# Five stream buffers instead of six, a twelfth kept weight chunk, and eleven zero stores moved from the output phase into the chain

## Chip, cores, metric

One core of one Trainium2 chip. The metric is the device time of one execution in microseconds (us), lower is better. A run more than 1.5% above the fastest of its kernel is called slow, and comparisons use fast runs.

## The reference

Two layers are applied twice, forward and backward, for one token (batch 1, sequence 1): attention over the last 4096 positions of a 32768-long cache (4 groups of 8 heads, head size 128, model width 1024), and an MLP of width 3584 with the mish activation. The kernel returns the output and the gradients of x, both caches and all weights.

```python
x = A_x
x = x + A(layernorm(x), k_cache, v_cache, wq, wo)   # called A1
x = x + B(layernorm(x), w1, b1, w2)                 # B2
x = x + A(layernorm(x), k_cache, v_cache, wq, wo)   # A3
x = x + B(layernorm(x), w1, b1, w2)                 # B4
# out, and the vjp with grad_out: dx, dK, dV, dwq, dwo, dw1, db1, dw2
```

Outside the window, dK and dV are zero: 28672 rows of 4 groups in each, 58.7 MB of zeros that the kernel has to write. It does so in 112 stores of 0.524 MB.

## The kernel before

The vector chain forward and backward (matrix-vector products) needs the weights several times; wq, K and V stay on the chip, 11 of 16 chunks of wo stay (NR), and everything else streams through a ring of six tiles (NB) of 0.524 MB. At the end the weight gradients, all outer products, are made and stored: the output phase. Zero stores are spread over the chain from POOL, each group behind a small copy ("gate") that makes it wait for a chosen value; the rest is stored from SP in the output phase. Cuts are marked.

```python
NB = 6          # ring tiles
NR = 11         # kept chunks of wo
# ...
def st_tile(shape):                  # the next ring tile, in turn
    s = free_order.pop(0)
    free_order.append(s)
    # ...
def bg_zeros(n, after):              # n zero stores from POOL, not before `after` is there
    if n:
        nc.gpsimd.tensor_copy(gate_t[:], after[:, 0:1])
    for _ in range(min(n, len(zero_jobs))):
        nc.gpsimd.dma_start(zero_job(1), zt[:])
# ... mlp_turn: B4 forward and backward over w1, seven blocks of two ring tiles each
for b in range(NBK):
    if b:
        bg_zeros(Z["B4"][b], dh_bf[:, lo0(b):])
    ws[b] = [w1_block(b, hh) for hh in range(2)]      # two loads
    # ... matrix-vector products of block b (PSUM "sm"): first the first half, then the second
    m = mish_exp(hps.cols(0, FB), FB)
    X(b, 0)                          # transposes of the first half, in place
    # ... mish and its derivative
    if b:
        M(b - 1)                     # backward product of block b-1: frees its two tiles
    X(b, 1)
    fill(4, ["wo", "V", "K", "wq"], None, True)       # transposes of kept weights
# ... zero stores of each stage
Z = dict(B2a=1, B2={0: 1, 4: 1, NW2 - 2: 3}, A3=14, B4=[2, 2, 2, 2, 2, 2, 5], A3c=6, A3d=28,
         B4w={1: 1, 4: 1, 7: 1, 10: 1, 12: 2}, W1=0, W1m=(2, 8, 13), A1c=3, A1d=18)
# ... output phase: zeros2(2) at five places, one at the end
```

In attention one ring tile is taken out for scratch, scores and p ("own").

## Time and profile before

| | before |
|---|---|
| time, median of the first 3 runs | 436.23 us (435.78 to 437.06) |
| span of the profiled run (fast) | 437.0 us |
| moved by DMA | 170.13 MB, 389 GB/s on average |
| last evacuation of PSUM ends | 416.1 us |
| from there to the end ("tail") | 20.9 us |

The lines behind these are in the prediction. For comparing kernels I cut the span at marks that every version has, read from the timeline: the start of the layernorms' ln (lnv) and of their backward sums (ab), the start of mish's exponential (u) for w1 blocks 0 and 6, and the end of the last evacuation of an outer product (ops).

### The profile page before, as it was taken

The page shows a single profiled execution, that of the slowest core. Times are in us where ns is not written, and L with a number is a line of the kernel's source. Part 1 is how long each engine was busy: PE and PEld are TensorE (multiplying, and loading weights), DVE is VectorE, ACT ScalarE, POOL GpSimd, SP SyncE. Part 2 cuts the span into 40 slices and gives each one's busy share as a digit, 9 for nine tenths or more (in the row PEclk, how much of TensorE's full clock was granted, in tenths as well). Part 3 has the DMA queues.
Part 4 walks back from the last instruction along what each step waited for, and adds up shares of the span by engine and source line. Part 5 has one row for each costly group of instructions (what it writes and reads, how often), then busy time and mean ns, then how long its engine had stood idle before and what let it go on. Part 6 is the DMA issues. An engine that isn't in the chain of part 4 may idle for free. (4 is left out here: it accounts for less than half of the span.)

```text
span 437.0 us, 11654 instructions
## 1 busy us (share of the span) xinstructions
PE 320.8 (73%) x5010; PEld 218.4 (50%) x5010; DVE 235.8 (54%) x489; ACT 212.5 (49%) x251; POOL 66.2 (15%) x167
## 2 busy tenths in 40 slices
PE   1566746387898998987999478888878797678800
PEld 0343515387474998974797477865431223112100
DVE  3134201086351666782474555556659899899900
ACT  1132100064242686875793242533548787698800
POOL 2000000010530221342242111022501010000000
PEclk9999555575695899997999555999885555555555
DMA  8999999999999799999999999999999999999996
GB/s 316 423 420 415 406 411 383 408 360 372 376 401 353 255 338 363 387 404 407 417 412 377 406 400 386 329 375 414 417 423 392 418 419 412 409 418 418 420 421 290
DMA packets 45057, 170.13 MB, mean 389 GB/s; under 512 B 4529, under 2 KB 11725, under 8 KB 38861
## 3 DMA queue, kind: packets, MB, share of 16 engines
q1 hardware_dynamic: 32752, 125.32, 73.0%
q0 software_dynamic: 12208, 44.06, 25.5%
q8 instruction: 39, 0.64, 0.6%
q14 instruction: 14, 0.11, 0.1%
q10 hardware_dynamic: 44, 0.01, 0.0%
HBM read 70.27 MB, written 99.10 MB: 388 GB/s over the span
## 5 line engine op out<-in xcount | busy, mean ns | idle before, releaser
L282 PEld LDWEIGHTS <-ring 128*128 128x128 bf16 (+2 forms) x1828 | 59.5, 101 | 35.9 <-DMA ring<-in_B_w_dram 11.9
L195 ACT COPY ring<-tps 128x1024 bf16<-128x1024 bf16 (+1 forms) x40 | 37.6, 963 | 27.4 <-PE tps L242 27.3
L185 POOL DMA_DIRECT2D out_dram<-zt x83 | 43.9, 531 | 40.6 <-DMA out_dram<-zt 34.7
L691 ACT COPY ring<-tps 128x1024 bf16<-128x1024 bf16 x28 | 28.3, 1012 | 31.6 <-PE tps L681 24.2
L704 DVE CUSTOM_DVE_ANT_0 ring<-ring,gbc 128x1024 bf16<-128x1024 bf16 x28 | 33.5, 1219 | 16.2 <-PE acc L282 15.1
L242 PE MATMUL tps<-ident_bf,ring 128*128 128x128 bf16 x528 | 38.9, 229 | 4.2 <-DMA ring<-in_B_w_dram 2.9
L282 PE MATMUL ops<-V 2*128 2x512 bf16 (+1 forms) x160 | 31.6, 602 | 7.3 <-DVE K L192 2.1
L195 ACT CAST wq_b<-ops 128x1024 bf16<-128x1024 f32 (+1 forms) x36 | 34.9, 1012 | 3.1 <-PE ops L282 3.0
L242 PEld LDWEIGHTS <-ring 128*128 128x128 bf16 x528 | 32.4, 102 | 6.1 <-DMA ring<-in_B_w_dram 2.5
L282 PEld LDWEIGHTS <-V 128*128 128x128 bf16 (+2 forms) x448 | 16.9, 102 | 33.6 <-issue 31.2
L195 ACT COPY K<-tps 128x1024 bf16<-128x1024 bf16 x17 | 16.8, 1027 | 30.1 <-PE tps L242 30.0
L192 DVE COPY ring<-tps 128x1024 bf16<-128x1024 bf16 (+1 forms) x30 | 19.7, 664 | 21.5 <-PE tps L242 21.5
L192 DVE CAST wq_b<-ops 128x1024 bf16<-128x1024 f32 (+1 forms) x28 | 30.6, 1119 | 0.7 <-PE ops L282 0.7
L282 PE MATMUL ops<-wo_b 2*128 2x512 bf16 x120 | 25.1, 526 | 5.6 <-DVE V L997 1.4
L681 PE MATMUL tps<-ident_bf,ring 128*128 128x128 bf16 x224 | 24.4, 276 | 0.7 <-DMA ring<-in_B_w_dram 0.7
L282 PE MATMUL acc<-a_pair,ring 128*128 128x16 bf16 x448 | 15.9, 172 | 11.5 <-DMA ring<-in_B_w_dram 10.7
L192 DVE COPY K<-tps 128x1024 bf16<-128x1024 bf16 x15 | 10.2, 689 | 24.2 <-PE tps L242 24.1
L192 DVE CAST K<-ops 128x1024 bf16<-128x1024 f32 x16 | 19.5, 1220 | 3.8 <-PE ops L282 3.5
L282 PEld LDWEIGHTS <-wo_b 2*128 2x128 bf16 (+1 forms) x232 | 9.1, 98 | 24.2 <-issue 20.8
L282 PE MATMUL q<-wq_b,nA_pair 128*32 128x512 bf16 x128 | 9.8, 425 | 14.9 <-DMA wq_b<-in_A_wq_dram 14.8
L242 PE MATMUL tps<-ident_bf,K 128*128 128x128 bf16 x256 | 20.2, 240 | 0.5 <-ACT K L195 0.3
L242 PEld LDWEIGHTS <-K 128*128 128x128 bf16 x256 | 17.1, 108 | 6.4 <-issue 5.4
(319 smaller groups left out, 560.7 us busy)
## 6 DMA issues: line engine op xcount, KB each, us to landing
out_dram<-zt POOLq DMA_DIRECT2D x83, 512.0 KB, 9.9
ring<-in_B_w_dram SPq DMA_DIRECT2D x42, 512.0 KB, 8.2
ring<-in_B_w_dram SPq DMA_DIRECT2D x32, 448.0 KB, 6.4
ring<-in_A_wo_dram SPq DMA_DIRECT2D x20, 512.0 KB, 8.0
out_dram<-wo_b SPq DMA_DIRECT2D x10, 1024.0 KB, 11.7
out_dram<-wq_b SPq DMA_DIRECT2D x10, 1024.0 KB, 14.9
out_dram<-zt SPq DMA_DIRECT2D x18, 512.0 KB, 11.0
wq_b<-in_A_wq_dram SPq DMA_DIRECT2D x8, 1024.0 KB, 21.1
```

Of the source, the lines that this page charges most:

```text
L185: nc.gpsimd.dma_start(zero_job(1), zt[:])
L192: nc.vector.tensor_copy(out_ap, in_ap)
L195: nc.scalar.copy(out_ap, in_ap)
L242: nc.tensor.transpose(ps[:, b, :], ap, ident_bf[:])
L282: nc.tensor.matmul(out_ap, lhsT=lhsT, rhs=rhs, start=start, stop=stop, skip_group_check=True, **kw)
L681: nc.tensor.transpose(self.ps[c][:, b, :], w[:, 1, b * P:(b + 1) * P], ident_bf[:])
L691: nc.scalar.copy(self.w[c][:, 1, :], self.ps.pop(c)[:].rearrange("p b c -> p (b c)"))
L704: nc.vector.tensor_tensor_reduce(out=w[:, 0, :], in0=w[:, 0, :], in1=gbc[:], scale=1.0, scalar=0.0, op0=ALU.mult, op1=ALU.add, accum_out=s ...
```

## The change

Intent: a twelfth chunk of wo is kept, so that it isn't streamed again in three of four passes; a ring tile pays for it. And the 11 zero stores of the output phase go into the chain, at places where DMA has holes, so that the output phase has less to store.

```diff
-NB = 6
-NR = 11
+NB = 5
+NR = 12
@@ mlp_fwd
         m = mish_exp(hacc.cols(0, TF), TF)
+        bg_zeros(Z["B2m"], m["y"])
         w2 = W2Pass(a_bf, "wg4")
@@
-    Z = dict(B2a=1, B2={0: 1, 4: 1, NW2 - 2: 3}, A3=14, B4=[2, 2, 2, 2, 2, 2, 5], ..., W1m=(2, 8, 13), A1c=3, A1d=18)
+    Z = dict(B2a=1, B2m=2, B2={4: 1, 10: 1, NW2 - 2: 3}, A3=17, B4=[3, 3, 3, 2, 2, 3, 5], ..., W1m=(2, 5, 8, 11, 13), A1c=3, A1d=19)
@@ output phase
-            16: [lambda: zeros2(2)],
-            22: [finish_rows, lambda: zeros2(2)],
-            26: [finish_rows, lambda: zeros2(2)],
-            32: [lambda: zeros2(2)],
-            40: [lambda: zeros2(2)],
+            22: [finish_rows],
+            26: [finish_rows],
```

(A third line chooses the staging tiles that the ring gives to the output phase; their number stays 14.)

More of the change, by code (lines that the diff above doesn't have):

```diff
@@ L1239, in after_stream @@
     def after_stream():
-        slots.extend(ring_b[:, i * 2048:(i + 2) * 2048] for i in range(0, NB, 2) if own["slot"] not in (i, i + 1))
+        slots.extend(ring_b[:, i * 2048:(i + 2) * 2048] for i in ((0, 2) if own["slot"] == 4 else (0, 3) if own["slot"] == 2 else (1, 3) if own["slot"] == 0 else (3,) if own["slot"] == 1 else (0,)))
     def after_v():
@@ L1251, in put_rows @@
         prep.pop(0)()
-    Z = dict(B2a=1, B2={0: 1, 4: 1, NW2 - 2: 3}, A3=14, B4=[2, 2, 2, 2, 2, 2, 5], A3c=6, A3d=28, B4w={1: 1, 4: 1, 7: 1, 10: 1, 12: 2}, W1=0, W1m=(2, 8, 13), A1c=3, A1d=18)
+    Z = dict(B2a=1, B2m=2, B2={4: 1, 10: 1, NW2 - 2: 3}, A3=17, B4=[3, 3, 3, 2, 2, 3, 5], A3c=6, A3d=28, B4w={1: 1, 4: 1, 7: 1, 10: 1, 12: 2}, W1=0, W1m=(2, 5, 8, 11, 13), A1c=3, A1d=19)
     x1 = None
```

## The prediction

> **What bounds the kernel now.** I read the 40 slices of the page first.
>
> ```profile
> PE   1566746387898998987999478888878797678800
> DVE  3134201086351666782474555556659899899900
> ACT  1132100064242686875793242533548787698800
> DMA  8999999999999799999999999999999999999996
> GB/s 316 423 420 415 406 411 383 408 360 372 376 401 353 255 338 363 387 404 407 417 412 377 406 400 386 329 375 414 417 423 392 418 419 412 409 418 418 420 421 290
> ```
>
> The kernel moves 170.13 MB in 437.0 us, 389 GB/s on average where the best slice reaches 423. The DMA row is 9 nearly everywhere, so DMA looks like the one bound; but GB/s falls to 255-390 in slices 8-16 and 25-26, and in the last ten slices DVE and ACT are as full as DMA. So I cut the span into stages with the table of windows (columns: length, busy time of PE, PEld, DVE, ACT and POOL with counts, clock, DMA share, GB/s).
>
> ```profile
> 60.00:112.00 52.00, 34.31 (x727) 30.07 (x726) 20.70 (x46) 14.88 (x17) 4.17 (x11) 0.57 1.01 381
> 112.00:147.00 35.00, 30.66 (x488) 20.78 (x489) 11.52 (x37) 10.44 (x20) 8.12 (x16) 0.75 1.00 374
> 147.00:150.00 3.00, 3.00 (x76) 3.00 (x74) 2.12 (x7) 1.93 (x3) 1.04 (x3) 1.00 0.13 41
> 150.00:180.00 30.00, 28.30 (x675) 27.60 (x673) 20.91 (x88) 23.85 (x30) 7.28 (x19) 1.00 0.99 356
> 238.00:264.00 26.00, 17.60 (x367) 16.77 (x364) 16.21 (x28) 11.63 (x12) 4.11 (x11) 0.58 1.02 394
> 264.00:292.00 28.00, 23.17 (x460) 22.07 (x461) 13.75 (x27) 10.52 (x13) 2.39 (x7) 0.84 0.99 358
> 338.00:416.00 78.00, 59.89 (x361) 16.61 (x359) 70.69 (x77) 64.51 (x69) 2.83 (x12) 0.50 1.02 416
> 416.00:434.00 18.00, 0.00 (x0) 0.00 (x0) 0.13 (x1) 0.01 (x1) 0.00 (x0) 0.50 0.98 409
> ```
>
> The rows are: first MLP forward (60-112); second attention forward (112-147); the second MLP's w1 blocks, forward and backward (147-180); after the attention backward, the second w2 pass (238-264) and first layer's w1 pass (264-292); the outer products of the output phase (338-416) and its tail, in which all compute is done and DMA drains (416-434). The output phase is full twice: DMA at 416 GB/s, and DVE at 70.69 of 78 us. What it waits for, the waits tell. In that window the lists of waits of DVE and of ACT hold no DMA at all, only each other and PE; so no evacuation is held by a staging buffer. The sync queue's last wait is for the final K stores:
>
> ```profile
> SPq L1425 <- DMA out_dram<-K: 15.0, 1, 15.0
> 416.19 4.39 SPq L1214 DMA_DIRECT2D out_dram<-K  x4
> out_dram<-K SPq DMA_DIRECT2D x4, 1024.0 KB, 14.0
> ```
>
> These K stores, 4 x 1.05 MB, can't be issued before the last evacuation (416), because one staging tile holds all of dK. In the chain I look for PE waiting for loads. Between 147 and 186 that is 0.7 us in two waits; between 238 and 292 it is 10.7 us:
>
> ```profile
> PE acc L282 <- DMA ring<-in_B_w_dram: 7.8, 7, 3.0
> PE tps L242 <- DMA ring<-in_B_w_dram: 2.9, 5, 0.9
> PE sm L282 <- DMA ring<-in_B_w_dram: 0.7, 2, 0.4
> ```
>
> **What the Trainium skill says.** Page "DMA: Bandwidth & Descriptors". Its section "Anatomy of one DMA" gives a fixed cost of about 2.0 us plus bytes at 436 GB/s: 3.2 us for a 524 KB zero store. The trace agrees: the one zero store at 149.1 us, with the queues empty, took 2.9 us. Section "Issuing engines are not separate DMA queues": transfers from SP and from POOL run on the same 16 DMA engines and interleave, so moving zero stores from SP to POOL buys no bandwidth; no slice here exceeds 423 GB/s, whichever queue feeds it. Section "Queues, rings and completion order": each DMA engine alternates between queues by the packet. A w1 block load has rows of 512 elements, 1 KB, a zero store rows of 4 KB, so a load beside zero stores should get far less than half. The trace fits: the same loads took a median of 5.1 us from issue to landing in 135-147, mostly without zeros, and 8.9 us in 146-190, with 19 zero stores.
>
> **The change, part by part.** A chunk or zero store is 0.524 MB, 1.26 us at 416 GB/s.
>
> Kept chunk: wo was loaded 11 + 4 x 5 = 31 times in chunks, now 12 + 4 x 4 = 28: 3 chunks, 1.57 MB, 3.8 us of DMA less, one each in the second forward and the two backward passes. On the engines it is nothing: the instruction order has 16 transposes moved from ring to kept tiles, and 2 of 10 multiply-reduces on DVE gone (1.22 us each, beside other work).
>
> Zero stores: 112 in all. Before, 83 from POOL in the chain, 18 from SP in the last attention backward, 11 from SP in the output phase. After: 94, 18 and 0. The 11 go to the first MLP (+2), second attention forward (+3), the w1 blocks (+4) and the last w1 pass (+2). In the output phase 11 x 1.26 = 13.9 us of DMA vanish. But not 13.9 us of time: compute ends at 416 either way. The wq store issued at 415.06 and the four K stores remain behind it: 5.24 MB, 12.6 us, started about 1.7 us after issue and about 1 us to the last receipt (estimates from the fixed cost above), so landing near 430.4 where now it is 435.6. **Gain at the end: 5.2 us.** The rest of the 13.9 us turns into idle DMA ahead of 416.
>
> Ring of five for six, with one of them scratch during attention: a load is issued when the tile five loads back is free.
> - First MLP: one load less is ahead when the layernorm starts, and one more zero store stands among the loads that count; 2 x 1.26 us against 52 us at 381 for 416 GB/s (4.4 us of slack). I put it at +1.
> - w1 blocks: each needs two tiles and keeps them until the next block is half done. With six tiles both halves of a block come free one block ahead. With five, the second half of block b+1 waits for the first half of block b-1, which M releases some 2.3 us into block b; blocks are 4.4 to 6.5 us long, landings took 8.9 us. DMA share is already 0.99. Added up to the end of the second w2 pass: four zeros, one half not prefetched, one wo chunk less, one prefetch less at the far end: +3 units, **+3.9 us**.
> - Last w1 pass: 2 zeros and a half more, 3.6 us; slack 28 us at 358 for 416, 3.9 us, but PE's 2.9 us of waits there (the transposes, tps, above) show that it is bound by loads already: +1.5.
> - Second attention forward: three zeros less one wo chunk; the 3 us with DMA share 0.13 after it swallow them: 0.
>
> Sum of the shift: +1 + 3.9 + 1.5 = +6.4. That counts nearly no idle DMA as usable. The gates that start each group of zeros (after the mish input, at chunk 4 and 10) are chosen for the holes, so I take about two thirds: **+4**. 436.2 - 5.2 + 4 = **435.0 us**.
>
> **Rivals.** (1) Everything fits in the holes: shift 0, 431.0 us. For it: about 15 us of unused bandwidth in 60-180 (each row's length times what its GB/s lack of 416); against it: the holes lie where the ring is full, and a smaller ring makes them larger. (2) The w1 blocks become bound by load latency: each of five blocks needs about 7 us (2.3 to the release, 4.6-5 to land) for the 5.7 it takes on average now (151.8 to 180.3 in PE's timeline), that is 5 x 1.3 = +6.5, and with contention from three zeros more; with the other terms about 440-442 us. For it: 8.9 us landings. Against: zeros are gated per block, so a late block also delays its competitors. (3) DMA bounds the output phase alone, as its 9s suggest: it would give back the whole 13.9 us and end near 426 with shift 4. Against: DVE and ACT never wait for a DMA there, and the K stores come last.
>
> **Range and chances.** Shift between -1.5 and +10 gives 429.5 to 441, eight in ten. Faster than 427.5 needs a shift below -3.5 or rival 3: 0.05. Slower than 445 needs +14: 0.03. Within 2%: 0.92.
>
> **What would show it.** Right: 168.56 MB moved; last evacuation at 420 +/- 3 instead of 416; last K landing 14-15 us after it instead of 19-20; a DMA hole ahead of it; more PE waits for ring loads at the w1 blocks than 0.7 us. Rival 1: last evacuation near 416. Rival 2: block period near 7 us and some 5 us of ring waits there. Rival 3: evacuations ending before 412. The prediction is wrong outright if evacuations begin to wait for staging tiles, of which the count stays 14, or if the clock granted to TensorE changes a stage.

## The result, and the profile after

| | before | after |
|---|---|---|
| time, median of 4 runs | 436.64 us (435.78 to 440.51) | 454.0 us (449.98 to 459.09) |
| ratio of fast runs | 1 | 1.0349 (95%: 1.0246 to 1.0452) |
| moved | 170.13 MB | 168.56 MB |

Ratios here are the mean time of one kernel's fast runs over that of the other's of the same rounds, so not quite the ratio of the medians. The change is 3.5% slower, outside the predicted range.

The two rows of the changed kernel's page that answer to the slices of before; this profiled run: slow (457.3 us).

```profile
DMA  8999999999999998899999999989998796999978
GB/s 325 420 421 415 408 366 342 375 359 315 376 411 368 366 346 306 315 386 337 412 413 400 381 379 374 316 296 378 415 411 350 298 418 260 392 411 423 378 317 367
```

Less is moved, at a lower rate, 369 GB/s on average; the holes are in the chain (slices 5 to 18 and 25 to 26, counted from 0, as in the prediction) and now in the output phase too. The end of the changed kernel, as a table of windows and the sync queue's timeline and last wait:

```profile
366.00:443.60 77.60, 59.56 (x359) 16.52 (x356) 70.31 (x77) 63.99 (x68) 2.74 (x12) 0.50 0.90 369
443.60:457.00 13.40, 0.00 (x0) 0.00 (x0) 0.00 (x1) 0.00 (x0) 0.00 (x0) 0.50 0.92 382
...
443.66 4.10 SPq L1215 DMA_DIRECT2D out_dram<-K  x4
...
SPq L1423 <- DMA out_dram<-K: 8.2, 4, 2.4
```

The evacuations do the same work in the same time as before (77.6 us here, 78.0 in the matching stretch before); DMA is no longer full beside them (369 for 416 GB/s); the last K stores follow at once, and the tail is 13.7 us instead of 20.9. So the output phase did about what was predicted. All the loss is earlier: the last evacuation ends at 443.6 instead of 416.1.

As that profile is a slow run, I use for the chain the profile of experiment e12, the changed kernel with nothing altered before the dK stores. Stage by stage (us; "A3 fwd" runs to the mish of block 0, "B4 blocks" from block 0 to block 6, "A3 bwd" from there to A3's backward layernorm, "w passes" are the second w2 pass and the last w1 pass, "outputs" runs from A1's backward layernorm to the last evacuation):

| stage | before | after (slow) | e12 (fast) | e12 - before |
|---|---|---|---|---|
| to B2's layernorm | 68.9 | 68.8 | 69.2 | +0.3 |
| B2 | 45.1 | 50.6 | 48.3 | +3.2 |
| A3 fwd | 34.5 | 34.3 | 34.0 | -0.5 |
| B4 blocks | 33.0 | 44.2 | 44.4 | +11.4 |
| A3 bwd | 53.6 | 52.7 | 52.0 | -1.6 |
| w passes | 56.8 | 65.8 | 65.2 | +8.4 |
| A1 bwd | 35.8 | 38.6 | 36.7 | +0.9 |
| outputs | 88.4 | 88.4 | 88.4 | 0 |
| tail | 20.9 | 13.7 | 11.4 (altered) | |
| span | 437.0 | 457.3 | 449.6 | |

Three stages lose 23.0 us, the blocks, the w passes, and B2; the others give 0.9 back, which leaves the 22.1 us by which e12's chain ends later. In all three PE stands still for ring loads. In B2 that was 11.1 us before and 12.8 in e12. These are PE's waits in the changed kernel, at the blocks (147 to 206 us) and in the w passes (250 to 320 us); before it was 0.7 us, and 7.8 + 2.9 us:

```profile
PE sm L282 <- DMA ring<-in_B_w_dram: 10.5, 4, 5.5
...
PE acc L282 <- DMA ring<-in_B_w_dram: 9.6, 7, 3.3
PE tps L242 <- DMA ring<-in_B_w_dram: 8.4, 7, 2.9
```

What one such wait looks like, in e12's timeline of PE at block 2 (start, length, what, and in brackets the idle time before it with its releaser):

```profile
159.83 0.19 PE L282 MATMUL sm<-b_b,ident_bf 128*128 128x64 bf16 x1
159.86 0.55 PE L282 MATMUL sm<-nB_pair,ring 128*128 128x16 bf16 x16
165.87 0.59 PE L282 MATMUL sm<-nB_pair,ring 128*128 128x16 bf16 x16 [5.46 <-DMA ring<-in_B_w_dram]
166.31 1.87 PE L242 MATMUL tps<-ident_bf,ring 128*128 128x128 bf16 x16
```

The first half of block 2 is there, the second comes 5.46 us late. The next 16 transposes take 1.87 us; in the block before they took 1.05. That is the half clock, granted after the idle time (the Trainium skill, "TensorE: Matmul & The Clock Gate", "Part 1: The HAM clock gate", says that idleness lowers the clock by half; the trace agrees, with a granted clock of 1.00 from 158 to 160 us and 0.50 from 165.8 to 168.2, and a mean of 0.88 in this stage for 1.00 before). So there are three suspects: too few tiles, zero stores that crowd out the loads, and the clock.

### The profile page after: what moved, and what is told of

It reads as the page before. It is cut to its first block, busy times and chain, and to the rows that moved or that the text cites.

```text
span 457.3 us, 11693 instructions
## 1 busy us (share of the span) xinstructions
PE 331.3 (72%) x5026; PEld 229.3 (50%) x5026; DVE 233.5 (51%) x484; ACT 213.7 (47%) x252; POOL 72.4 (16%) x181
## 2 busy tenths in 40 slices
DMA packets 45344, 168.56 MB, mean 369 GB/s; under 512 B 4560, under 2 KB 11756, under 8 KB 39788
## 5 line engine op out<-in xcount | busy, mean ns | idle before, releaser
L185 POOL DMA_DIRECT2D out_dram<-zt x94 | 49.7, 532 | 41.1 <-DMA out_dram<-zt 34.2
L242 PE MATMUL tps<-ident_bf,ring 128*128 128x128 bf16 x512 | 42.8, 248 | 8.4 <-DMA ring<-in_B_w_dram 8.4
L242 PEld LDWEIGHTS <-ring 128*128 128x128 bf16 x512 | 36.3, 112 | 10.1 <-DMA ring<-in_B_w_dram 7.7
L282 PEld LDWEIGHTS <-V 128*128 128x128 bf16 (+2 forms) x448 | 16.9, 102 | 33.6 <-issue 31.2
L192 DVE COPY ring<-tps 128x1024 bf16<-128x1024 bf16 (+1 forms) x28 | 18.3, 662 | 24.9 <-PE tps L242 24.8
L681 PE MATMUL tps<-ident_bf,ring 128*128 128x128 bf16 x224 | 26.3, 292 | 0.7 <-DMA ring<-in_B_w_dram 0.7
L192 DVE CAST wo_b<-ops 128x1024 bf16<-128x1024 f32 (+1 forms) x18 | 20.7, 1186 | 4.5 <-PE ops L282 4.5
L282 PEld LDWEIGHTS <-wo_b 128*128 128x128 bf16 (+1 forms) x280 | 10.4, 100 | 23.1 <-issue 19.9
L681 PEld LDWEIGHTS <-ring 128*128 128x128 bf16 x224 | 20.0, 132 | 1.2 <-DMA ring<-in_B_w_dram 0.8
```

What stands on the lines that cost most here:

```text
L192: nc.vector.tensor_copy(out_ap, in_ap)
L242: nc.tensor.transpose(ps[:, b, :], ap, ident_bf[:])
L282: nc.tensor.matmul(out_ap, lhsT=lhsT, rhs=rhs, start=start, stop=stop, skip_group_check=True, **kw)
L681: nc.tensor.transpose(self.ps[c][:, b, :], w[:, 1, b * P:(b + 1) * P], ident_bf[:])
```

## The experiments

Twelve kernels ran, on three chips; each is compared with the kernel before on the same chip, whose median there was 438.7 to 440.3 us. Stages are from the profiled run of each, which was fast except for e4.

| run | ratio (95%) | B2 | B4 blocks | w passes | tail | span |
|---|---|---|---|---|---|---|
| before | 1 | 45.1 | 33.0 | 56.8 | 20.9 | 437.0 |
| e1 ring only | 1.0255 (1.0173-1.0338) | 51.4 | 39.2 | 61.0 | 19.9 | 451.1 |
| e2 zeros only | 1.0078 (1.0048-1.0108) | 44.6 | 40.8 | 62.8 | 14.0 | 442.0 |
| e3 no output zeros | 0.9839 (0.9767-0.9911) | 43.8 | 32.3 | 56.1 | 14.0 | 428.8 |
| e4 no block zeros | 1.0289 (1.0143-1.0435) | 49.0 | 33.5 | 65.8 | 25.8 | 458.8 (slow) |
| e5 holes | 0.9937 (0.9908-0.9967) | 45.3 | 36.9 | 59.9 | 13.9 | 436.4 |
| e6 holes, dK halves | 0.9956 (0.9926-0.9985) | 45.1 | 35.4 | 59.9 | 14.4 | 433.3 |
| e7 warm | 1.0367 (1.0300-1.0434) | 49.1 | 44.4 | 63.1 | 13.7 | 452.4 |
| e8 last w1 pass only | 1.0012 (0.9967-1.0057) | 44.0 | 34.2 | 58.6 | 18.1 | 436.6 |
| e9 five tiles | 1.0289 (1.0234-1.0343) | 49.9 | 38.4 | 61.9 | 25.4 | 451.9 |
| e10 no w-pass zeros | 1.0350 (1.0279-1.0421) | 49.3 | 44.5 | 54.5 | 20.8 | 452.2 |
| e11 holes 2 | 0.9885 (0.9844-0.9927) | 44.5 | 33.6 | 58.9 | 15.0 | 432.4 |
| e12 after, dK halves | 1.0288 (1.0215-1.0361) | 48.3 | 44.4 | 65.2 | 11.4 | 449.6 |

### e1: the ring alone, and e2: the zero stores alone

```diff
 # e1: from the changed kernel
-Z = dict(..., B2m=2, B2={4: 1, 10: 1, ...}, A3=17, B4=[3, 3, 3, 2, 2, 3, 5], ..., W1m=(2, 5, 8, 11, 13), ...)
+Z = dict(..., B2={0: 1, 4: 1, ...}, A3=14, B4=[2, 2, 2, 2, 2, 2, 5], ..., W1m=(2, 8, 13), ...)   # and zeros2 as before
 # e2: from the kernel before, the reverse; NB = 6, NR = 11 stay
```

> The changed kernel (twelve kept chunks, ring of five) with the zero stores where they were before (83 in the chain, 11 in the output phase). Theory A (the ring of five makes PE wait for loads): the chain still ends 12 to 20 us later than the 416 of before, PE still waits 5 us or more for ring loads at the w1 blocks, time 448 to 456. Theory B (the zero stores moved into the chain delay it, the ring is nearly free): last evacuation within 4 us of 416, time 435 to 440.

> The kernel before (eleven kept chunks, ring of six) with the zero stores placed as in the changed kernel. Theory A: chain later by 3 to 6 us at most (DMA volume of 11 zero stores less what falls in holes), the tail after the last evacuation 14 us instead of 21, time 431 to 437. Theory B: chain later by 15 us or more, time 445 to 452.

e1 took 450.1 us for 440.3 (+2.6%), e2 443.4 (+0.8%); the sum, 3.3%, is close to the 3.5% of the whole change. So both parts cost, and the ring costs more: theory A holds for e1. For e2 neither theory does: the zero stores alone delayed the last evacuation by 12 us (428.0 for 416.1), between the 3 to 6 of theory A and the 15 of theory B, and gave 7 back in the tail. Stage by stage the two parts don't just add: at the blocks e1 lost 6.2 and e2 7.8 us, and both together (e12) 11.4. The blocks in a table of windows, one row each for before, e1, e2 (columns as in the prediction):

```profile
148.60:181.60 33.00, 31.30 (x746) 30.60 (x744) 23.41 (x94) 25.88 (x33) 9.92 (x24) 1.00 0.95 341
```

```profile
154.30:193.50 39.20, 32.36 (x745) 31.91 (x743) 23.45 (x94) 25.89 (x33) 10.52 (x25) 0.95 0.88 308
```

```profile
148.50:189.40 40.90, 33.57 (x748) 33.17 (x746) 23.53 (x95) 25.95 (x33) 12.09 (x28) 0.87 0.96 343
```

The two differ in kind. With five tiles (e1) the stage is longer although no zero store was added there, and the rate falls to 308 GB/s with a DMA share of 0.88: DMA stands idle for part of the time while PE waits for a load. With four more zero stores and six tiles (e2) the rate stays at 343 GB/s, and the stage is longer because more goes through it, 14.0 MB for 11.3 (rate times length).

### e3: what the output phase can give

```diff
-            16: [lambda: zeros2(2)],        # and at 22, 26, 32, 40
-    zeros2(1000)
-    assert not zero_jobs
+    assert len(zero_jobs) == 11             # 11 stores left out: result wrong on purpose
```

> The kernel before without the 11 zero stores of its output phase (those parts of the outputs are left unwritten, wrong on purpose). If the last K stores set the end, as the prediction said: last evacuation still near 416, tail 14 to 16 us instead of 21, time 430 to 432 (5.2 us gained). If DMA alone bounds the output phase: 13.9 us gained, 422 to 424.

The time was 432.1 us (ratio 0.9839); the result was wrong in dV, as it must be. Tail and evacuations of the profiled run:

```profile
326.40:414.80 88.40, 68.96 (x402) 18.60 (x401) 80.99 (x98) 72.80 (x77) 4.55 (x21) 0.50 0.91 374
414.80:428.80 14.00, 0.00 (x0) 0.00 (x0) 0.02 (x1) 0.00 (x0) 0.00 (x0) 0.50 0.88 365
```

The tail is 14.0 us, not the 7.0 that taking away 13.9 us of DMA time from 20.9 would leave: half of the stores taken away became idle DMA (374 GB/s in place of 413, over the same 88.4 us) ahead of the last evacuation. The last K stores set the end once the queue before them is empty. 6.9 us is all that the output phase has to give; the prediction said 5.2. This bounds what any placement of the zero stores can win while dK is stored at once.

### e4: zero stores beside the block loads

```diff
-B4=[3, 3, 3, 2, 2, 3, 5]
+B4=[0, 0, 0, 0, 0, 0, 5]      # from the changed kernel; these 16 stores go to the output phase
```

> The changed kernel with no zero store beside w1 blocks 0 to 5; these 16 go to the output phase. If zero stores starve the late load of each block (contention), PE's waits for ring loads at the w1 blocks fall from 10.5 us to under 3, and the stage from mish of block 0 to that of block 6 from 44 us to 34-37. If the latency of the late load alone does it, the waits stay above 5 us and the stage above 39. Time: chain 8 us earlier than in the changed kernel in the first case, tail back at some 20 us, so 448 to 451.

PE's waits at the blocks fell to 2.2 us and the stage to 33.5 us, as long as with six tiles before. The profiled run is slow, which can't have made the stage shorter. Window, and the median landing time of the w1 loads during the first blocks, of e4:

```profile
154.40:187.90 33.50, 31.26 (x747) 30.80 (x744) 23.45 (x94) 25.99 (x32) 3.01 (x7) 1.00 0.50 164
...
ring<-in_B_w_dram SPq DMA_DIRECT2D x6, 512.0 KB, 4.3
```

and the same two of e12, with the 16 stores:

```profile
151.40:195.80 44.40, 33.77 (x747) 33.41 (x745) 23.47 (x94) 26.02 (x32) 12.63 (x29) 0.88 0.95 338
...
ring<-in_B_w_dram SPq DMA_DIRECT2D x8, 512.0 KB, 5.3
```

So five tiles are enough for the blocks when the loads have DMA to themselves, half of whose time is then idle. Landing took 5.3 us in e12 and 8.9 before: with six tiles a load is issued early and may take long, with five it is issued late and has to be quick.

Do the stores cost by standing in front of a late load, or by the DMA time that they take? The rows shown answer in part. Length times DMA share is the time for which DMA was busy at the blocks (shares in these tables run up to 1.03, so it is good to some 3%):

| at the blocks | length, us | DMA busy, us | moved, MB |
|---|---|---|---|
| before | 33.0 | 31 | 11.3 |
| e1, five tiles | 39.2 | 34 | 12.1 |
| e2, zero stores | 40.9 | 39 | 14.0 |
| e4, five tiles, no zero stores here | 33.5 | 17 | 5.5 |
| e12, both | 44.4 | 42 | 15.0 |

In e12 DMA has 42 us of work, so as long as this work lies in the stage it can't take 33.5 us, whatever the order of the transfers. The 3.8 MB that it moves more than before are 11.0 us at the 341 GB/s of before, and the loss is 11.4. So at the blocks of the changed kernel the zero stores cost mainly the DMA time that they take. A load that comes late although DMA has time is what e1 shows, with 12% of DMA idle. That single stores in front of single loads cost more than their volume in e12 is argued and not shown. The time of e4 did not improve (1.0289, and its runs scatter from 448.8 to 460.8), as the 16 stores came back in a tail of 25.8 us, more than the 20 that I expected.

### e7: is the lowered clock a cost of its own?

```diff
             for t in range(TD):
+                if t == HT and b in (2, 3, 4, 6):
+                    warm({2: 20, 3: 5, 4: 9, 6: 6}[b])     # matmuls on idle data
```

> The changed kernel with some 40 extra matmuls (about 8.6 us at full clock) on idle data put ahead of the second half of w1 blocks 2, 3, 4 and 6, where PE waited 10.5 us for loads. If the lowered clock after each wait is a cost of its own: granted clock 1.0 through the blocks, stage from block 0 to block 6 near 42 us instead of 44.2 although work was added, later stages as in the changed kernel. If the clock does not matter: stage 44 to 47 us.

40 matmuls were put where PE waited for the late halves. PE's waits for ring loads went from 10.5 to 3.2 us, the stage stayed at 44.4 us and the ratio at 1.0367 (1.0349 for the changed kernel). The stage was no shorter and no longer, though it had work added: in this stage the loads set the pace. The granted clock rose only to 0.93, so this was no clean test of a clock of 1.0; a cost of the clock in other stages is not excluded. A1 bwd, whose work e2 leaves as it was, took 35.8 us before at a granted clock of 0.90 and 37.3 us in e2 at 0.83. Other traces go the same way: 32.6 us at 1.00 (e9), 36.7 at 0.87 (e12), 38.5 at 0.82 (e5), 38.6 at 0.76 (the changed kernel's slow run). So length and clock go together there; which of them makes the other no experiment settles.

### e9: five tiles without the twelfth chunk

```diff
 # from the kernel before: in B2, at the B4 blocks and in the w passes one of six tiles is left unused
+    spare = free_order.pop()
     x2, sB2, wg4 = mlp_fwd(x1, "B2", gcolb)
+    free_order.append(spare)        # the same around mlp_turn; own tile kept through the w passes
-            pre.extend(w2_load(c) for c in range(NB - 1))
+            pre.extend(w2_load(c) for c in range(NB - 2))
```

> The kernel before with eleven kept chunks and its zero stores, but only five of its six ring tiles used in the MLP stages (first MLP, w1 blocks, second w2 pass, last w1 pass). If the number of tiles is what costs: the losses of the ring-only run return stage by stage: first MLP 50 us instead of 45, block stage 38-40 instead of 33, stage from A3-backward to B2-backward 60-62 instead of 57; ratio 1.022 to 1.035. If it was the twelfth kept chunk (its extra column matmuls and transposes): every stage as before, ratio 0.995 to 1.005.

The ratio is 1.0289, and the losses of e1 return in the same stages: B2 49.9 (51.4), blocks 38.4 (39.2), w passes 61.9 (61.0). So it is the number of tiles and not the twelfth chunk. What the chunk saves can't be told from these: the intervals of e1 and e9 overlap. Nor do these three stages make up all of e9's time: its A1 bwd was 3.2 us shorter (32.6) and its tail 4.5 us longer (25.4) than before, and I followed up neither. B2 shows the tile's effect most plainly, having no other change: before, and e9.

```profile
69.00:114.10 45.10, 30.28 (x684) 27.55 (x684) 20.04 (x46) 14.79 (x18) 3.44 (x9) 0.58 1.00 377
```

```profile
69.10:118.90 49.80, 31.18 (x684) 28.58 (x684) 20.17 (x46) 14.88 (x17) 3.44 (x9) 0.57 0.93 334
```

The same 684 matmuls take about the same busy time at the same clock, and nearly the same bytes (16.6 and 17.0 MB, rate times length) move at 334 instead of 377 GB/s.

### e8 and e10: the w passes

```diff
 # e8: from the kernel before, two stores moved from the output phase
-W1m=(2, 8, 13)
+W1m=(2, 5, 8, 11, 13)
 # e10: from the changed kernel, 11 stores moved to the output phase
-B4w={1: 1, 4: 1, 7: 1, 10: 1, 12: 2}, W1=0, W1m=(2, 5, 8, 11, 13)
+B4w={}, W1=0, W1m=()
```

> The kernel before with two zero stores moved from the output phase into the last w1 pass (chunks 5 and 11), nothing else. Zeros-only took 62.7 us instead of 56.7 in the stage from A3-backward to B2-backward. If these two zero stores do that themselves: 60 to 63 us here. If it was backlog from the zero stores at the w1 blocks: 56 to 58.5 us here, and ratio 0.993 to 0.998.

> The changed kernel without the 11 zero stores of the second w2 pass and the last w1 pass; they go to the output phase. Stage from A3-backward to B2-backward is 65.8 us in the changed kernel, 56.7 before. If zero stores beside the loads make it: 52 to 57 us; if the ring of five alone does it by its latency: 60 us or more. The chain then ends 9 to 13 us earlier, the tail is back at some 20 us, so total 449 to 453.

e8: 58.6 us for 56.8, and no gain in time (1.0012), though its tail was 2.8 us shorter. So two stores explain a third of e2's six. The rest is backlog, and e2's trace shows it: 16 zero stores were issued in its w passes, 10 before and 13 in e8, while A3's backward stage, after the blocks, issued 30 instead of 34. e10: 54.5 us, with five tiles less than before with six. Rows of before, e12, e10:

```profile
235.20:291.90 56.70, 43.47 (x885) 41.14 (x882) 31.56 (x59) 23.63 (x26) 7.04 (x19) 0.73 1.00 376
```

```profile
247.80:313.10 65.30, 46.69 (x886) 44.45 (x883) 31.82 (x60) 23.67 (x26) 8.51 (x23) 0.68 0.99 362
```

```profile
252.80:307.40 54.60, 41.20 (x889) 38.55 (x886) 31.66 (x60) 23.68 (x26) 0.00 (x0) 0.84 0.90 313
```

Again it is the zero stores beside the loads that fill the stage. The total did not improve (1.0350, where I expected 449 to 453 us and the median was 455.5): the 11 stores came back as a tail of 20.8 us.

### e5, e6, e11, e12: can the gain of the output phase be had?

```diff
 # e5: from the kernel before; six zero stores stay in the output phase
-B2={0: 1, 4: 1, NW2 - 2: 3}, A3=14
+B2m=2, B2={4: 1, 10: 1, NW2 - 2: 3}, A3=17
 # e6: e5, and e12: the changed kernel, with dK stored in two halves
-    dkv(sA3["ds"], r3("q3"), sA1["ds"], r3("q1"), out_2, False)
+    dkv(sA3["ds"], r3("q3"), sA1["ds"], r3("q1"), out_2, True)
 # e11: from the kernel before; seven stay in the output phase
-B2={0: 1, 4: 1, NW2 - 2: 3}, A3=14
+B2m=2, B2={4: 1, 9: 2, 11: 2, NW2 - 2: 3}, A3=13
```

> The kernel before (ring of six, eleven kept chunks) with only those zero stores moved that cost no time in the zeros-only run: the two of the first MLP and the three of the second attention forward; six stay in the output phase. If the loss came from the zero stores at the w1 blocks and in the last w1 pass: block stage 33 us, A3-backward to B2-backward stage 57 us as before, tail after the last evacuation 20.9 - 5 x 1.26 = 14.6 us, ratio 0.985 to 0.988. If moving any zero stores ahead delays the chain by its DMA volume: no gain, ratio 0.997 to 1.003.

> As the holes kernel, with dK stored in two halves, so that only 2.1 MB instead of 4.2 MB wait for the last evacuation. If the tail is now set by what DMA has queued (six zero stores still there), nothing changes against the holes kernel (tail 14 to 15 us, ratio 0.985 to 0.988); if the K stores alone set it, the tail falls by 5 us to 9.5 and the ratio to 0.973 to 0.977.

> The kernel before with four zero stores moved from the output phase, one from the second attention forward, all into the first MLP, ahead of the second attention's (13 there instead of 14, seven left in the output phase). If a zero store is free as long as it is done before the w1 blocks load: block stage 33 us as before, tail 20.9 - 4 x 1.26 = 15.9, ratio 0.986 to 0.991, better than the 0.9937 of the holes kernel. If it is only moved waiting: block stage above 35 and no better than 0.994.

> The changed kernel with dK stored in two halves. If its end is set by the last K stores alone (DMA has holes ahead of the last evacuation): tail 13.7 - 5.0 = 8.7 us and time 5 us below the changed kernel, 447 to 450, ratio 1.020 to 1.026. If queued stores set it: tail 13 to 14 and no change.

e5 gained 0.6%, half of what was expected. Its five stores were free in B2 (45.3 us) and in A3's forward pass itself (34.3), but the blocks after it took 36.9 us. They moved 13.4 MB for 11.3 before (rate times length), at a DMA share of 1.02: what the three stores of A3 pushed back had to go through there, most of it loads (6.6 MB on the sync queue for 4.9). e6 shows no change against e5, as expected where the queue and not the last store sets the end. e11 puts the stores earlier, into B2's second half, and takes one away from A3. Its blocks:

```profile
147.80:181.40 33.60, 31.75 (x747) 31.66 (x745) 23.53 (x94) 25.71 (x32) 9.88 (x24) 0.95 0.99 352
```

33.6 us, nearly as before, a tail of 15.0, and 433.5 us for 438.7: ratio 0.9885 (0.9844 to 0.9927). It beats the kernel before, though by less than 2%; 2.1 us were lost in the w passes, which I had not expected and did not follow up.

e12 was a miss: the tail fell to 11.4 and not to 8.7 us. Its sync queue:

```profile
424.66 4.11 SPq L1215 DMA_DIRECT2D out_dram<-K  x4
428.87 8.59 SPq L1195 DMA_DIRECT2D out_dram<-wq_b  x4
438.26 4.28 SPq L1215 DMA_DIRECT2D out_dram<-K  x4
```

In the last 13.6 us before the last evacuation 2.1 MB of K and 4.2 MB of wq stores are issued, 6.3 MB, while 5.7 MB fit at 416 GB/s: the first half comes too late for a free DMA, and I take it that part of it is still queued. The 0.6 MB too much are 1.5 us, so this leaves 1.2 of the 2.7 us open.

## Why the prediction was wrong

- **The output phase: right.** Evacuations unchanged (88.4 us in nearly every version), 168.56 MB, the K stores at the end, a hole in DMA ahead of them. The gain at the end was 7.2 us for 5.2: the two overheads that I added for issue and receipt were too large (1.7 + 1 us, although the fixed cost that they were to come from is 2.0). Rival 3 fell with e3.
- **The shift of the chain: wrong, and this is the step that failed.** "Sum of the shift: +1 + 3.9 + 1.5 = +6.4 ... so I take about two thirds: +4". It was +22.1 (e12, fast). By terms: B2, put at +1, was +3.2; the blocks and what follows to the end of the second w2 pass, put at +3.9 through volume, began with +11.4 at the blocks alone; the w passes, of which I had the last at +1.5, were +8.4 together; A3's forward pass, 0, was right for the stage itself (-0.5), but its three stores were paid for in the blocks after it (36.9 us for 33.0 in e5, 35.4 in e6). Rival 1, no shift, fell with this: the last evacuation came at 438.2 (e12).
- **Why it was too small.** The slack was misread. I took what a row's GB/s lack of 416 for unused bandwidth ("about 15 us of unused bandwidth in 60-180"). But three of the four rows behind it show a DMA share of 0.99 to 1.01; idle DMA is only in the row at 147-150, 0.87 of 3 us, 2.6 us. At the blocks DMA, busy 95% of the time, moved 341 GB/s before, and loads nearly alone move no more when it is busy (e4: 164 GB/s at a share of 0.50, that is 328). So a unit of 0.524 MB costs 1.5 us there and not 1.26, and 7 units came where I had netted 3 up to the end of the second w2 pass: A3's backward stage, which then moves less, gave back 1.6 us only. With one tile less, further, the same loads go out later, and the rate falls (334 for 377 GB/s in B2, e9). I had put no cost on that in B2 beyond a load and a store.
- **Rival 2 was nearer.** It said five blocks of about 7 us; in e12 the five from block 1 to block 6 took 10.8, 7.6, 7.3, 6.8 and 7.4. Its mechanism, blocks bound by the latency of a load, is what e1 shows, where DMA has idle time: 8.0, 6.7, 6.5, 6.3 and 7.1, +6.2 us for its +6.5. In the changed kernel DMA time fills the stage as well (e4's table), so there the number alone doesn't confirm it. I set it aside because "zeros are gated per block, so a late block also delays its competitors". The gate does not take away the stores that go with the loads of that very block. Its total of 440-442 us was still too low, as it held the other terms small.
- **The two thirds.** I cut the sum because the placing of the stores looked chosen with care. That was no evidence. e2 shows that the same placing costs 0.8% even with six tiles. Nor was there ground for a chance of 0.03 for more than 445 us, with rival 2 on the page and its contention left without a number.

## What to carry to other kernels

A transfer buffer that seems spare on average may be what lets a load be issued early enough; count from the release of a tile to the use of its next content, beside what else is queued then, before giving one away. Before calling bandwidth unused, look at the DMA share beside the GB/s: a stage can be full at 341. Background stores paid where they were done before the stretch of loads with a deadline (e11); beside it (e2) they cost more than they gave, and running into it (e5) they lost half of the gain. And before moving work out of a full phase, see what ends it: here half of the work taken away left only idle DMA.

## What the Trainium skill lacked or had wrong

- "DMA: Bandwidth & Descriptors", "Queues, rings and completion order", says that engines alternate between queues by the packet. It does not say what that does to the time of a load: w1 loads landed in 5.1 us (median) with few zero stores beside them and in 8.9 us with 19 (the kernel before, 135 to 147 and 146 to 190 us).
- "Trainium Kernel Development and Optimization", "Best Practices", has double-buffering, and that bubbles can mean that on-chip memory ran out, but nothing on how many buffers are enough: five ring tiles instead of six, with the same transfers, cost 2.9% (e9).
- "TensorE: Matmul & The Clock Gate", "Part 4: PE-mode transpose", says that the full clock does not engage for transposes. Here 192 transposes in a row, made with nc.tensor.transpose, took 11.11 us, 58 ns each, and the granted clock was 1.00 from 218 to 228 us (the kernel before; timeline, and window):

```profile
217.50 11.11 PE L242 MATMUL tps<-ident_bf,wq_b 128*128 128x128 bf16 x192
...
218.00:228.00 10.00, 10.00 (x178) 9.98 (x176) 7.18 (x11) 10.00 (x13) 4.08 (x8) 1.00 1.03 413
```
